# The last token tile's output product in two column halves, with its gate's products four places earlier in the order list

## Chip, cores and metric

One core of one Trainium2 chip runs the whole program. The metric is the device time of one execution in microseconds. Before the change three runs gave 260.70, 261.08 and 261.57 us, so the median is 261.08 us. One further execution was taken with the hardware profiler, and every instruction time below is from that one.

## What is computed

The inputs are `q`, `k`, `v`, `a_re`, `a_im` of shape (4, 8, 768, 48): batch, heads, sequence, head dimension. A complex gate `a`, capped at magnitude 0.999, drives a recurrence whose read-out `y` is `x` for a feed-forward part with a gated residual:

```python
S_re, S_im = (new_re + kv, new_im)                 # for each time step t
y[:, :, t] = np.einsum('bhd,bhde->bhe', q[:, :, t], S_re)
...
g, val = x @ w_gate, x @ w_val                     # x: 3072 tokens x 384
ffn_out = gelu(g) * val @ w_out                    # 384 -> 1536 -> 384
res_gate = 1.0 / (1.0 + np.exp(-(x @ w_res)))
return (x + res_gate * ffn_out).astype(np.float32)
```

The output is 3072 x 384 in float32.

## The kernel before

**Tiling.** The sequence is cut into chunks of 128 steps. One pair (batch, chunk) is a tile of 128 tokens, 24 in all. Tiles are worked on in 14 units, mostly two tiles at a time; the last two units hold one tile each: unit 12 is batch 2, chunk 5, and unit 13 is batch 3, chunk 5. `prepare` makes the decayed features of a unit, `attend` makes `x`, and `forward` makes the output. The loops over units call these three in turn, but that isn't the order in which instructions stand.

**The order.** Each call of `add` (L138) records a step: its engine, its kind, a function that issues its instructions, and the values that it reads and writes. Steps are numbered as they are recorded. `ORDER` (L41 to L105) is a list of these numbers, written out by hand, and `Plan.run` (L159) issues the steps in just that order. Each engine has its own queue, so a step's place matters against the other steps of its engine. `PLACE` (L30) maps some step numbers to an engine other than the one the code gives as a default. `Plan.run` also picks buffers: eight PSUM banks (`pb`) and three output tiles (`ot`) go round. For the kinds in `PORT` (L26), `otx` among them, it adds a wait that keeps such steps of DVE and of POOL one after the other. Waits between the engines are put in by the framework, from which tiles an instruction reads and writes.

**The end of `forward`** (L563 to L627), for one tile of 128 tokens:

- six rounds of gate and value products (L592, PE), GELU (L597, ACT) and gating (L598, DVE) give `h2`, 1536 x 128 in bf16;
- step kind `res`, three products with `wr` into a bank of its own (L607, PE), and `tanh` into `sg` (L609, ACT);
- step kind `out`, three steps of four products each (L618, PE), which add up in one bank of 128 x 384 float32. `lo` is 0, 4 and 8, and the third step closes the sum;
- step kind `ot`, the gate product `(sg + 1) * out` (L622, DVE). The factor one half of the sigmoid has been put into the gating of `h2`;
- step kind `otx`, the sum with `x` (L625, on POOL unless `PLACE` says DVE);
- step kind `store`, one DMA of 192 KB from SP's queue (L627).

The tile that finishes last is that of unit 12. `PLACE` puts its `otx` (step 1376) on DVE. The end of `ORDER` reads, with unit 13's steps (1378 and up) among unit 12's:

```
... 1445, 1368, 1443, 1369, 1372, 1446, 1373, 1447, 1370, 1448, 1374, 1371, 1449, 1375, 1376, 1377
```

Here 1372, 1373 and 1374 are the three `out` steps of unit 12, 1370 is its `res`, 1371 its `tanh`, 1375 its `ot`, 1376 its `otx` and 1377 its `store`. 1445 and 1446 are `out` steps of unit 13, 1447 is its `ot`, 1448 its `otx` and 1449 its `store`. On PE the last 23 products are therefore: unit 12 `lo` 0 and unit 13 `lo` 4 and 8 with unit 12 `lo` 4 (16 products in all), `res` of unit 12 (3), and unit 12 `lo` 8 (4).

After the last step the program closes: SP waits for every DMA semaphore and every engine's semaphore in turn, and then the engines meet at a barrier (all at the launching line, L665).

Of the kernel before, what the change touches and what calls it, by code (L numbers as in the profile page):

```python
# [15 lines left out]
OP = mybir.AluOpType  # L16
# [11 lines left out]


PLACE = {  # L30
    33: "DVE", 50: "DVE", 64: "ACT", 105: "DVE", 114: "DVE", 116: "POOL", 121: "DVE", 131: "DVE", 134: "ACT", 190: "DVE",
    191: "DVE", 213: "DVE", 221: "ACT", 223: "DVE", 225: "ACT", 230: "ACT", 245: "DVE", 305: "DVE", 306: "DVE", 323: "POOL",
    330: "DVE", 340: "DVE", 342: "ACT", 353: "DVE", 435: "ACT", 438: "ACT", 456: "DVE", 460: "DVE", 469: "DVE", 539: "DVE",
    551: "ACT", 554: "POOL", 555: "POOL", 562: "DVE", 570: "ACT", 572: "DVE", 576: "DVE", 599: "DVE", 654: "DVE", 667: "ACT",
    671: "POOL", 678: "DVE", 688: "DVE", 690: "ACT", 692: "DVE", 695: "ACT", 771: "DVE", 783: "ACT", 787: "POOL", 804: "DVE",
    806: "ACT", 811: "ACT", 817: "DVE", 831: "DVE", 872: "DVE", 899: "DVE", 902: "POOL", 903: "POOL", 943: "DVE", 1014: "POOL",
    1015: "POOL", 1022: "DVE", 1033: "ACT", 1041: "DVE", 1088: "DVE", 1124: "POOL", 1125: "POOL", 1143: "ACT", 1204: "DVE",
    1298: "DVE", 1314: "DVE", 1324: "ACT", 1325: "POOL", 1376: "DVE", 1386: "DVE", 1396: "ACT", 1397: "POOL", 1401: "DVE",
    1448: "DVE",
}  # L40
ORDER = [  # L41
# [63 lines left out]
]  # L105


# [19 lines left out]
class Plan:  # L127
# [10 lines left out]
    def add(self, eng, kind, fn, reads=(), writes=(), size=1, act=None):  # L138
        deps = set()
        for v in reads:  # L140
            deps.update(v.writers)
        for v in writes:
            deps.update(v.writers)
            deps.update(v.readers)
        stores = [v.store for v in list(reads) + list(writes) if v.store is not None]
        stores = sorted(set(stores), key=stores.index)
        t = Step(eng, kind, fn, deps, stores, size, act)
        t.index = len(self.steps)
        for v in writes:
            v.writers, v.readers = [t], []  # L150
        for v in reads:
            if t not in v.writers:
                v.readers.append(t)
        for x in stores:
            x.users.append(t)
        self.steps.append(t)
        return t
# [30 lines left out]
def kernel(  # L188
# [13 lines left out]
    nc = tc.nc  # L202
# [3 lines left out]
    DM = H * D  # L206
    FF = moe_w_gate.shape[1]
    KF = DM // 128
    NF = FF // 128
# [6 lines left out]
    NU = len(units)  # L216
    where = {bc: (p, i) for p, u in enumerate(units) for i, bc in enumerate(u)}
    size = [len(u) for u in units]

    ctx.enter_context(tc.manual_schedule())  # L220
    cst = ctx.enter_context(tc.tile_pool(name="cst", bufs=1))
# [26 lines left out]
    wo = cst.tile([128, NF, DM], BF, name="wo")  # L248
# [76 lines left out]
    on = {"DVE": nc.vector, "POOL": nc.gpsimd, "ACT": nc.scalar}  # L325
    add = plan.add

    def place(default):

        return PLACE.get(len(plan.steps), default)  # L330
# [6 lines left out]
    W = {}  # L337
# [226 lines left out]
    def forward(p):  # L564
        s, n = st[p], size[p]
        s["xT"], s["h2"] = Buf("xT"), Buf("h2")
        xT = [s["xT"].part() for _ in range(n)]
        for i in range(n):
            if p >= PE_X:
                add("SP", "dX", lambda i=i: nc.sync.dma_start(  # L570
                    out=s["xT"].tile[:, :, i, :], in_=s["x"].tile[:, i].rearrange("p h d -> p (h d)"), transpose=True), [s["xi"][i]], [xT[i]])
# [3 lines left out]
            def f(i=i, xp=xp):  # L575
                xp.make([128, KF, 128], BF)
                for k_ in range(KF):
                    nc.tensor.transpose(out=xp.tile[:, k_, :],
                                        in_=s["x"].tile[:, i].rearrange("p h d -> p (h d)")[:, k_ * 128:(k_ + 1) * 128], identity=ident)
# [3 lines left out]
        h2 = []  # L583
        for m in range(NF // 2):
            gp, vp, hh = Bank(), Bank(), s["h2"].part()
            h2.append(hh)
            for name, w_, o_ in (("wg", wg, gp), ("wv", wv, vp)):
# [11 lines left out]
                out=hv(), in0=hv(), scalar=0.5, in1=vp.tile, op0=OP.mult, op1=OP.mult), [vp], [hh], n)  # L599
        sg = [Buf("sg") for _ in range(n)]  # L600
# [9 lines left out]
                [rp], [sg[i]], 1, "G")  # L610
        for i, (b, c) in enumerate(units[p]):
            op_, ot = Bank(), Buf("ot")
            for lo in range(0, NF, 4):
                def f(i=i, lo=lo, op_=op_):
                    if lo == 0:
                        op_.make([128, DM])
                    for k_ in range(lo, lo + 4):
                        nc.tensor.matmul(out=op_.tile, lhsT=s["h2"].tile[:, k_, i * 128:(i + 1) * 128], rhs=wo[:, k_, :],  # L618
                                         start=(k_ == 0), stop=(k_ == NF - 1))
                add("PE", "out", f, [h2[lo // 2], h2[lo // 2 + 1], W["wo", lo]], [op_])  # L620
            ti = b * NC + c
            add("DVE", "ot", lambda i=i, op_=op_, ot=ot: nc.vector.scalar_tensor_tensor(  # L622
                out=ot.tile, in0=sg[i].tile, scalar=1.0, in1=op_.tile, op0=OP.add, op1=OP.mult), [sg[i], op_], [ot])
            e8 = place("POOL")
            add(e8, "otx", lambda i=i, ot=ot, e8=e8: on[e8].tensor_tensor(  # L625
                out=ot.tile, in0=ot.tile, in1=s["x"].tile[:, i].rearrange("p h d -> p (h d)"), op=OP.add), [s["xi"][i]], [ot])
            add("SP", "store", lambda ot=ot, ti=ti: nc.sync.dma_start(out=out[ti * 128:(ti + 1) * 128, :], in_=ot.tile), [ot], [])  # L627

    weights()
    for p in range(NU):  # L630
# [39 lines left out]
```

## Time and profile before

| what | value |
|---|---|
| median of three runs | 261.08 us (260.70 to 261.57) |
| the profiled execution | 261.98 us |
| its span, first to last instruction | 260.2 us |
| granted TensorE clock, mean | 0.974 |
| busy share PE, DVE, ACT, POOL | 85%, 87%, 81%, 35% |
| chain that ended last, by engine | PE 60%, DVE 19%, DMA 7%, SP's queue 5% |
| L618, `out` products 128x384, 288 of them | 55.5 us |
| L622, `ot` 128x384 on DVE, 24 of them | 13.1 us, 547 ns each |
| L625, `otx` 128x384 on POOL, 18 of them | 16.9 us, 941 ns each |
| L625, `otx` 128x384 on DVE, 6 of them | 556 ns each |
| stores on SP's queue, 24 of 192 KB | 2.5 us to landing (median) |

The profile follows one execution. PE, DVE, ACT and POOL are the compute engines, PEld is PE's weight load, SP issues DMAs, and a `q` behind an engine's name means its sequencer, which waits and issues. The chain of waits is followed back from the last instruction to whatever released each step. The timeline lists instructions with start and duration in microseconds.

### The profile page before, as it was taken

What the parts mean: (1) busy time and instruction counts of PE and PEld (TensorE: products, weight loads), DVE (VectorE), ACT (ScalarE), POOL (GpSimd) and SP (SyncE); (2) the same over time, 40 slices, a digit from 0 to 9 for tenths busy, and PEclk for the clock granted to TensorE, in tenths of its full rate; (3) what the DMA queues carried; (4) which work ended last, traced back from release to release, by engine and by line L of the source; (5) the groups of instructions that cost most, each with busy time, mean ns of one, the idle gap of its engine ahead of it and who ended that gap; (6) DMA issues with size and microseconds to landing.
All of it is one profiled execution on the core that took longest, in us unless ns stands there. A gap on an engine that the chain in (4) does not pass through costs nothing.

```text
span 260.2 us, 6343 instructions
## 1 busy us (share of the span) xinstructions
PE 222.3 (85%) x2415; PEld 174.7 (67%) x2415; DVE 225.7 (87%) x401; ACT 211.3 (81%) x354; POOL 90.4 (35%) x116
## 2 busy tenths in 40 slices
PE   0233842877999999999999999999999999999993
PEld 0011532757878877887887778768778778877881
DVE  2789999997999999999999999999999976573463
ACT  4899999998999999999999999797999932532330
POOL 1022266594611662486626177006020230101100
PEclk9999975799999999999999999999999999999999
DMA  8999999999999998999986779779789539201311
GB/s 140 188 186 186 188 185 167 205 181 217 152 183 185 164 199 161 192 178 183 214 147 121 153 155 168 181 145 232 131 134 222 97 88 170 75 3 35 113 40 60
DMA packets 162174, 39.83 MB, mean 153 GB/s; under 512 B 155616, under 2 KB 162144, under 8 KB 162144
## 3 DMA queue, kind: packets, MB, share of 16 engines
q1 hardware_dynamic: 157696, 35.53, 78.1%
q0 software_dynamic: 4448, 3.90, 9.7%
q8 instruction: 19, 0.31, 0.6%
q14 instruction: 11, 0.09, 0.1%
HBM read 31.26 MB, written 4.72 MB: 138 GB/s over the span
## 4 chain that ended last, share of the span: by engine, by line
PE 60%; DVE 19%; DMA 7%; SPq 5%; issue 4%; POOL 1%; ACT 0%; DVEq 0%; POOLq 0%; ACTq 0%
PE pb L592 30%; PE pb L618 16%; SPq L374 5%; PE pb L607 3%; PE pb L360 3%; PE pb L522 3%; DMA t<-fr 2%; PE pb L492 2%; DVE h L598 2%; DMA k<-in_k_dram 2%; DMA ai<-in_a_im_dram 2%; DVE fQ L475 2%; DVE Qe L470 2%; DVE ll L408 1%; DMA vf<-in_v_dram 1%
## 5 line engine op out<-in xcount | busy, mean ns | idle before, releaser
L597 ACT ACTIVATE h<-pb 128x512 bf16<-128x512 f32 (+1 forms) x84 | 41.1, 550 | 23.5 <-PE pb L592 23.1
L592 PE MATMUL pb<-xT,wg 128*128 128x256 bf16 (+1 forms) x504 | 56.0, 257 | 1.2 <-DVE U L552 0.9
L592 PE MATMUL pb<-xT,wv 128*128 128x256 bf16 (+1 forms) x504 | 57.0, 257 | 0.0
L618 PE MATMUL pb<-wo,h 128*128 128x384 bf16 x288 | 55.5, 326 | 0.0
L598 DVE SCALAR_TENSOR_TENSOR h<-h,pb 128x512 bf16<-128x512 bf16 (+1 forms) x84 | 48.0, 601 | 7.3 <-ACT h L597 4.6
L592 PEld LDWEIGHTS <-wg 128*128 128x128 bf16 x504 | 43.1, 98 | 8.1 <-issue 1.6
L592 PEld LDWEIGHTS <-wv 128*128 128x128 bf16 x504 | 42.2, 98 | 6.1
L639 ACT ACT_TABLE_LOAD x34 | 43.6, 1283 | 1.3 <-PEq L654 0.7
L525 DVE TENSOR_TENSOR am<-pb,mask 128x512 bf16<-128x512 f32 x48 | 31.6, 680 | 4.5 <-PE pb L522 4.3
L618 PEld LDWEIGHTS <-h 128*128 128x128 bf16 x288 | 26.0, 97 | 13.8 <-issue 0.3
L625 POOL TENSOR_TENSOR ot<-ot,x 128x384 f32<-128x384 f32 x18 | 16.9, 941 | 46.1 <-issue 19.9
L444 POOL TENSOR_TENSOR tl<-t,th 128x768 fp32r<-128x768 f32 (+1 forms) x9 | 13.2, 1479 | 22.7 <-DVE Gb L554 14.3
L522 PE MATMUL pb<-QT,KT 96*128 96x128 bf16 x192 | 16.7, 219 | 2.7 <-DVE KT L335 2.4
L622 DVE SCALAR_TENSOR_TENSOR ot<-sg,pb 128x384 f32<-128x384 f32 x24 | 13.1, 547 | 6.3 <-PE pb L618 6.2
L360 PE MATMUL pb<-lh,ut_hf 128*128 128x384 f16 x24 | 8.6, 360 | 11.1 <-DVE lh L406 11.1
L398 POOL TENSOR_TENSOR t<-t,ai 128x768 f32<-128x768 f32 (+1 forms) x9 | 14.7, 1637 | 8.8 <-DMA ai<-in_a_im_dram 3.5
L522 PEld LDWEIGHTS <-KT 96*128 96x128 bf16 x192 | 12.7, 97 | 6.5 <-DVE KT L335 2.9
L492 PE MATMUL pb<-ident,fK 128*128 128x128 bf16 x112 | 10.7, 252 | 6.8 <-DVE fK L475 6.0
L609 ACT ACTIVATE sg<-pb 128x384 f32<-128x384 f32 x24 | 11.9, 499 | 5.2 <-PE pb L607 3.2
L607 PE MATMUL pb<-wr,xT 128*128 128x384 bf16 x72 | 15.6, 326 | 0.3 <-DVE am L525 0.2
L334 ACT CAST x<-pb 128x384 bf16<-128x384 f32 x19 | 9.2, 482 | 6.4 <-PE pb L536 6.1
L360 PE MATMUL pb<-th,ut_hf 128*128 128x384 f16 x24 | 8.6, 359 | 6.4 <-DVE th L335 6.0
(89 smaller groups left out, 467.3 us busy)
## 6 DMA issues: line engine op xcount, KB each, us to landing
ar<-in_a_re_dram SPq DMA_DIRECT2D x24, 192.0 KB, 4.6
ai<-in_a_im_dram SPq DMA_DIRECT2D x24, 192.0 KB, 4.7
q<-in_q_dram SPq DMA_DIRECT2D x24, 192.0 KB, 4.6
k<-in_k_dram SPq DMA_DIRECT2D x24, 192.0 KB, 4.1
vf<-in_v_dram SPq DMA_DIRECT2D x24, 192.0 KB, 4.0
out_dram<-ot SPq DMA_DIRECT2D x24, 192.0 KB, 2.5
wg<-in_moe_w_gate_dram POOLq DMA_DIRECT2D x6, 192.0 KB, 7.1
wv<-in_moe_w_val_dram POOLq DMA_DIRECT2D x6, 192.0 KB, 6.2
```

Of the source, the lines that this page charges most:

```text
L360: nc.tensor.matmul(out=bank.tile, lhsT=ones, rhs=x[:, i * DM:(i + 1) * DM], start=(j == 0), stop=(j == 1))
L398: add(e1, "tai", lambda: on[e1].tensor_tensor(out=F("t"), in0=F("t"), in1=flat(T("ai"), n), op=OP.mult), [s["ai"]], [s["t"]], n)
L492: nc.tensor.transpose(out=tp.tile[:, h, :], in_=s[g].tile[:, i * H + h], identity=ident)
L522: nc.tensor.matmul(out=ap.tile[:, h, :], lhsT=kT.tile[0:DD, u * H // 2 + h, :], rhs=qT.tile[0:DD, u * H // 2 + h, :], start=True, stop=True)
L525: add("DVE", "am", lambda u=u, am=am, ap=ap: nc.vector.tensor_tensor(out=am.tile[:, u * H // 2:(u + 1) * H // 2, :], in0=ap.tile, in1=mask ...
L592: nc.tensor.matmul(out=o_.tile[:, u, :], lhsT=w_[:, k_, (2 * m + u) * 128:(2 * m + u + 1) * 128], rhs=s["xT"].tile[:, k_, 0:n].rearrange(" ...
L597: add("ACT", "gelu", lambda gp=gp, hv=hv: nc.scalar.activation(out=hv(), in_=gp.tile, func=AF.Gelu), [gp], [hh], n, "G")
L598: add("DVE", "h", lambda vp=vp, hv=hv: nc.vector.scalar_tensor_tensor(out=hv(), in0=hv(), scalar=0.5, in1=vp.tile, op0=OP.mult, op1=OP.mul ...
L607: nc.tensor.matmul(out=rp.tile, lhsT=s["xT"].tile[:, k_, i, :], rhs=wr[:, k_, :], start=(k_ == 0), stop=(k_ == KF - 1))
L618: nc.tensor.matmul(out=op_.tile, lhsT=s["h2"].tile[:, k_, i * 128:(i + 1) * 128], rhs=wo[:, k_, :], start=(k_ == 0), stop=(k_ == NF - 1))
L625: add(e8, "otx", lambda i=i, ot=ot, e8=e8: on[e8].tensor_tensor(out=ot.tile, in0=ot.tile, in1=s["x"].tile[:, i].rearrange("p h d -> p (h d ...
L639: plan.run(ORDER, lambda table: nc.scalar.preload_act_table_set(ACT_SETS[table]), after)
```

## The change

Only the tile of unit 12 (`TAIL = 12`) is treated differently. Its third `out` step becomes two steps of kind `outh`, each of four products over 192 of the 384 columns, into the two halves of the same bank. Then come two `ot` steps of 192 columns on DVE, two sums with `x` of a new kind `oth`, of 192 columns, the first on POOL and the second on DVE, and two stores of 128 x 192. `oth` isn't in `PORT`. Since unit 12 records four steps more, every later number in `ORDER` and `PLACE` goes up by four; the entry that put unit 12's `otx` on DVE is gone, and the new steps take the defaults. Beyond the numbering, the tail of `ORDER` changes: `res` and `tanh` of unit 12 (1370, 1371) now stand ahead of its second `out` step.

```diff
-    1437, 1357, 1442, 1365, 1366, 1445, 1368, 1443, 1369, 1372, 1446, 1373, 1447, 1370, 1448, 1374, 1371, 1449, 1375, 1376,
-    1377,
+    1441, 1357, 1446, 1365, 1366, 1449, 1368, 1447, 1369, 1372, 1450, 1370, 1371, 1373, 1451, 1452, 1374, 1375, 1453, 1376,
+    1377, 1378, 1379, 1380, 1381,
...
+            cols = [slice(0, DM)] if p != TAIL else [slice(0, DM // 2), slice(DM // 2, DM)]
+            acc, res = [op_], [ot]
             for lo in range(0, NF, 4):
...
+                if lo == NF - 4 and len(cols) > 1:
+                    acc, res = [Val(op_.store) for _ in cols], [Val(ot.store) for _ in cols]
+                    for x in acc:
+                        x.writers = list(op_.writers)
+                for x, sl in zip(acc, cols if len(acc) > 1 else [slice(0, DM)]):
+                    def f(i=i, lo=lo, op_=op_, sl=sl):
...
+                            nc.tensor.matmul(out=op_.tile[:, sl], lhsT=s["h2"].tile[:, k_, i * 128:(i + 1) * 128], rhs=wo[:, k_, sl],
+                                             start=(k_ == 0), stop=(k_ == NF - 1 and sl.stop == DM))
+                    add("PE", "out" if len(acc) == 1 else "outh", f, [h2[lo // 2], h2[lo // 2 + 1], W["wo", lo]], [x])
             ti = b * NC + c
...
+            for j, (x, y, sl) in enumerate(zip(acc, res, cols)):
+                add("DVE", "ot", lambda i=i, op_=op_, ot=ot, sl=sl: nc.vector.scalar_tensor_tensor(
+                    out=ot.tile[:, sl], in0=sg[i].tile[:, sl], scalar=1.0, in1=op_.tile[:, sl], op0=OP.add, op1=OP.mult), [sg[i], x], [y])
+            for j, (x, y, sl) in enumerate(zip(acc, res, cols)):
+                e8 = place("POOL" if j == 0 else "DVE")
+                add(e8, "otx" if len(cols) == 1 else "oth", lambda i=i, ot=ot, e8=e8, sl=sl: on[e8].tensor_tensor(
+                    out=ot.tile[:, sl], in0=ot.tile[:, sl], in1=s["x"].tile[:, i].rearrange("p h d -> p (h d)")[:, sl], op=OP.add), [s["xi"][i]], [y])
+            for j, (x, y, sl) in enumerate(zip(acc, res, cols)):
+                add("SP", "store", lambda ot=ot, ti=ti, sl=sl: nc.sync.dma_start(
+                    out=out[ti * 128:(ti + 1) * 128, sl], in_=ot.tile[:, sl]), [y], [])
```

In the new numbering 1374 and 1375 are the two `outh` steps, 1376 and 1377 the two gate products, 1378 (POOL) and 1379 (DVE) the two sums, 1380 and 1381 the two stores, and 1451, 1452 and 1453 are `ot`, `otx` and `store` of unit 13.

More of the change, by code (lines that the diff above doesn't have):

```diff
@@ L30 @@
 PLACE = {
[L31 to L39, printed above, removed]
+    33: "DVE", 50: "DVE", 64: "ACT", 105: "DVE", 114: "DVE", 116: "POOL", 121: "DVE", 131: "DVE", 134: "ACT", 190: "DVE", 191:
+    "DVE", 213: "DVE", 221: "ACT", 223: "DVE", 225: "ACT", 230: "ACT", 245: "DVE", 305: "DVE", 306: "DVE", 323: "POOL", 330:
+    "DVE", 340: "DVE", 342: "ACT", 353: "DVE", 435: "ACT", 438: "ACT", 456: "DVE", 460: "DVE", 469: "DVE", 539: "DVE", 551:
+    "ACT", 554: "POOL", 555: "POOL", 562: "DVE", 570: "ACT", 572: "DVE", 576: "DVE", 599: "DVE", 654: "DVE", 667: "ACT", 671:
+    "POOL", 678: "DVE", 688: "DVE", 690: "ACT", 692: "DVE", 695: "ACT", 771: "DVE", 783: "ACT", 787: "POOL", 804: "DVE", 806:
+    "ACT", 811: "ACT", 817: "DVE", 831: "DVE", 872: "DVE", 899: "DVE", 902: "POOL", 903: "POOL", 943: "DVE", 1014: "POOL", 1015:
+    "POOL", 1022: "DVE", 1033: "ACT", 1041: "DVE", 1088: "DVE", 1124: "POOL", 1125: "POOL", 1143: "ACT", 1204: "DVE", 1298:
+    "DVE", 1314: "DVE", 1324: "ACT", 1325: "POOL", 1390: "DVE", 1400: "ACT", 1401: "POOL", 1405: "DVE", 1452: "DVE",
 }
@@ L218 @@
     size = [len(u) for u in units]
+    TAIL = 12
     ctx.enter_context(tc.manual_schedule())
@@ L612, in forward @@
             op_, ot = Bank(), Buf("ot")
+            cols = [slice(0, DM)] if p != TAIL else [slice(0, DM // 2), slice(DM // 2, DM)]
+            acc, res = [op_], [ot]
             for lo in range(0, NF, 4):
[L614 to L619, printed above, removed]
@@ L620, in forward @@
-                add("PE", "out", f, [h2[lo // 2], h2[lo // 2 + 1], W["wo", lo]], [op_])
-            ti = b * NC + c
[L622 to L626, printed above, removed]
@@ L627, in forward @@
-            add("SP", "store", lambda ot=ot, ti=ti: nc.sync.dma_start(out=out[ti * 128:(ti + 1) * 128, :], in_=ot.tile), [ot], [])
+                if lo == NF - 4 and len(cols) > 1:
[4 more added lines that the diff above has]
+                    def f(i=i, lo=lo, op_=op_, sl=sl):
+                        if lo == 0:
+                            op_.make([128, DM])
+                        for k_ in range(lo, lo + 4):
+                            nc.tensor.matmul(out=op_.tile[:, sl], lhsT=s["h2"].tile[:, k_, i * 128:(i + 1) * 128], rhs=wo[:, k_, sl],
+                                             start=(k_ == 0), stop=(k_ == NF - 1 and sl.stop == DM))
+                    add("PE", "out" if len(acc) == 1 else "outh", f, [h2[lo // 2], h2[lo // 2 + 1], W["wo", lo]], [x])
```

46 rows, old and new, of the table ORDER are left out of this document.

## The prediction

> **What bounds the kernel now.** I read the chain of waits first, and of it only the end, since the change touches only the last tile.
>
> ```profile
> 253.88 0.81 PE pb L618 x5
> 254.69 0.49 PE pb L607 x3
> 255.18 0.66 PE pb L618 x4
> 255.84 0.04 DVEq L622
> 255.88 0.04 issue
> 255.93 0.56 DVE ot L622
> 256.49 0.02 issue
> 256.51 0.56 DVE ot L625
> ```
>
> PE runs without a gap to 255.84 us; then come the gate product, the sum with x and a store, one behind the other. What follows is in the timeline (first line: SP's queue), in the DMA view of 257.0 to 259.6 us (40 slices of 0.065 us), and in the closing waits of SP, line L665, asked for 257.2 to 258.2 and for 258.5 to 259.2 us:
>
> ```profile
> 257.10 0.33 SPq L627 DMA_DIRECT2D out_dram<-ot  x1
> ```
>
> ```profile
> DMA  0000000000000048999999520000000000000000
> out_dram<-ot SPq DMA_DIRECT2D x1, 192.0 KB, 1.9
> ```
>
> ```profile
> L665 SPq EVENT_SEMAPHORE  x9: 17/28/28, 257.5 to 258.0; - x9
> ```
>
> ```profile
> L665 SPq EVENT_SEMAPHORE  x1: 28/28/28, 259.0 to 259.0; - x1
> ```
>
> The store is issued at 257.10, its packets move from 257.91 to about 258.5 (0.6 us), it has landed 1.9 us after the issue, at 259.0, and the span ends 1.2 us later, at 260.2. Nine closing waits are through long before the landing, and a single one is left when it comes. So from PE's end there are 4.36 us of tail: 0.09 to the gate product, 1.14 to the sum's end, 0.03 to the store, 1.9 to the landing, 1.2 of closing. Only these can change.
>
> **Part 1, PE.** `res` and `lo` 4 swap places: three and four products of 0.163 us each (0.49/3, 0.66/4). Their sum stays. Neither waits: the last gating of h2 ends at 252.97 in the timeline, before either. The sixteen products ahead and unit 13's `ot`, `otx` and store keep their places. The tanh (0.49 us, from 255.22 to 255.71 before) ends about 0.65 us sooner, but it wasn't last: the gate product waited for PE to 255.84. If that cover went, nothing is lost, as the tanh only gets earlier. Gain 0. Four products of 384 columns become eight of 192. Products of 128 columns, each with its own weight load, stand in the chain at 6.70 us for 120, 0.056 each; at 384 it is 0.163. 192 lies on that line at 0.083, so eight take 0.66: cost +0.01 at most. Below nothing is excluded, the columns being the same.
>
> **Part 2, when the gate product can start.** The gain would be that the first half starts after four of the eight products, 0.33 us before PE's end. The built program speaks against it: of the two DVE gate products, the first waits for PE, ACT and a DMA, the second names no wait at all. The second needs the second half's products, so the first's wait already covers these. Both start after all eight. Gain 0.
>
> **Part 3, DVE.** One gate product of 0.553 and one sum of 0.557 become two of 192 columns and one of 192. The group rows have L598 (the same operation) at 410 ns for 256 columns and 678 for 512, 1.05 ns a column; so 192 takes 0.553 - 192 x 1.05 ns = 0.35 us, the sum 0.36. Independent DVE instructions of L598 follow each other closer than their duration (eight of 0.41 in 2.74 us, 0.34 apart, so 0.07 overlaps). First product 255.94 to 256.29, second 256.22 to 256.57, and its sum 256.59 to 256.95 if nothing stops it. That is 0.12 us earlier than before (257.07).
>
> **Part 4, POOL.** The first half's sum goes to an engine whose 128x384 sum has a median of 912 ns, and whose 128x768 subtraction (L444) takes 1641; 1.9 ns a column, so 192 takes 0.912 - 0.365 = 0.55 us (ends: 0.46, half of 912, and 0.91). From the end of a gate product on DVE to POOL's start the timeline has 0.12 (223.25 to 223.37), 0.13 (243.21 to 243.34) and 0.23 (238.59 to 238.82). With 0.13: start 256.42, end 256.97. SP follows a POOL end by 0.03 (239.73 to 239.76). So the first half store is issued at 257.00, only 0.10 before the whole one was.
>
> **Part 5, the second store behind the first on SP.** The added wait is the first store's for POOL, and the second store is queued behind it. Two stores that were both ready, one right behind the other:
>
> ```profile
> 245.94 0.33 SPq L627 DMA_DIRECT2D out_dram<-ot  x1
> ```
>
> ```profile
> 246.36 0.38 SPq L627 DMA_DIRECT2D out_dram<-ot  x1
> ```
>
> They are 0.42 apart, and the issue cost is the same for half a tile as far as the rows go (0.33 for 128 rows of 1536 bytes; 0.37 at the least for loads with 1024 rows of 192 bytes). So the second store is issued at 257.42, 0.32 later than before. DVE's half, ready at 256.95, waits 0.47 there. Of the 1.9 us to landing 0.6 are packets. Half the bytes take 0.3 at the same rate; the loads' packets of 192 bytes take 20.6 ns each by queue q1's share (78.1% of 16 engines over 260.2 us, 157,696 packets), those of 1536 bytes 0.6 x 16/128 = 75 ns, so 768 bytes lie near 44 ns or 0.35 us for 128 packets on 16 engines. Landing after 1.9 - 0.6 + 0.35 = 1.65 (ends 1.6 and 1.9): at 259.07, against 259.0. Net **+0.07** (ends -0.1 and +0.45).
>
> **Part 6, the closing waits.** The DMA semaphores of SP's queue are eight, taken in turn. The last store of before has number 7, and the closing waits go from 0 to 7, so only its own was left at the landing. The change adds one DMA: the last store now has number 0 (its row in the built program waits for DMAHW0, where the half before it waits for DMAHW7). Numbers 1 to 7 are then waited for after it has landed. The nine closing waits quoted run from 257.5 to 258.0, by their starts 0.06 apart. Seven more behind the landing cost 7 x 0.06 = **+0.42** (ends: 0, should they be taken faster when all are met; 0.45).
>
> **Sum.** 0.01 + 0.07 + 0.42 = +0.50 us. The profiled execution took 261.98, its span 260.2 and 1.78 around it, which nothing here touches: 262.48. It is 0.90 above the median of the runs shown, 261.08; the tail doesn't hang on that, so on the median's scale I forecast **261.6**. The bounds of the terms give -0.1 to +0.9.
>
> **A rule that speaks against the change.** While POOL's sum ran from 243.34, a gate product ran on DVE from 243.37:
>
> ```profile
> 243.34 0.91 POOL L625 TENSOR_TENSOR ot<-ot,x 128x384 f32<-128x384 f32 x1 [3.62 <-issue]
> 243.37 0.55 DVE L622 SCALAR_TENSOR_TENSOR ot<-sg,pb 128x384 f32<-128x384 f32 x1 [0.15 <-PE pb L618]
> ```
>
> Both took what they take alone. But there DVE read one operand from PSUM. DVE's second sum reads both from SBUF, and no row shows that beside a POOL sum, since `PORT` keeps those apart and `oth` isn't in it. The Trainium skill, page "SBUF — State Buffer", section "Who interferes with whom", says that a VectorE instruction with two SBUF inputs contends with a GpSimd instruction that reads SBUF, and that the second to start is blocked until the first is through. The pair quoted agrees with its other half, that one SBUF input doesn't contend. By that rule, if POOL is first (256.42 against 256.59), DVE's sum runs from 256.97 to 257.33, still ahead of the second store's turn at 257.42: the sum stays.
>
> **Rivals.**
> 1. *DVE takes the operands first* (slower): if POOL starts later than 256.59, 0.30 and not 0.13 after the first product (the longest gap seen is 0.23), and the two then exclude each other, POOL's sum starts at 256.97 and ends at 257.52, the stores go at 257.55 and 257.97, the landing is at 259.62, the closing 0.42 later: +1.05 us, **262.1**. Against it: the gap must be longer than any row's. Chance 0.13. The rule of the Trainium skill's page "SBUF — State Buffer" would give just this.
> 2. *The closing waits cost nothing*, or the second store lands a little sooner: +0.1 us, **261.2**. For it: the waits' spacing was seen while nothing waited behind them. Chance 0.20.
> 3. *The first half does start early*, though the built waits say otherwise: first product at 255.61, POOL's sum 256.09 to 256.64, stores at 256.67 and 257.09, landing 258.74, closing 0.42 later: +0.16, **261.2**. Not faster even so. Chance 0.05.
> 4. *The halves gain*: a POOL sum of 0.46, a store that lands in 1.6, closing for nothing: -0.1, and with a lucky draw of runs faster by more. Chance 0.04.
>
> The forecast has the rest, 0.58.
>
> **Chances and range.** Runs of this kernel differ by 0.87 us, and about 0.3% (0.78 us) is what a measurement can tell from no change. The forecast's +0.5, with 0.35 for its terms and for a median of few runs, passes +0.78 in a fifth of its cases (0.12); rival 1 does in nearly all (0.12); the others hardly (0.02). Slower 0.26, faster 0.03, within 0.3% 0.71. The range takes in rivals 2 and 3 below and rival 1 above: 260.9 to 262.3.
>
> **What would show it.** In the profile after: the two gate products start 0.28 apart behind PE's end (Part 2; 0.3 before it, and rival 3 holds). The first sum on POOL takes 0.55 and its store goes near 257.0 if the rest of the span is unmoved (Part 4). The two stores are 0.42 apart, and PE's end to the last landing is 3.23 us against 3.16 (Part 5). After the last landing seven or eight closing waits of L665 instead of one, and 1.6 us to the end of the span instead of 1.2 (Part 6). PE's end to the end of the span is 4.9 us against 4.36. It is wrong if POOL starts after DVE's sum, if half a store lands as late as a whole one, or if the span before 253 us moves, which nothing in the change asks for: no other instruction changes its place.

## The result, and the profile after

The changed kernel takes 261.79 us (median of nine runs, 261.58 to 262.29) against 260.72 us for the kernel before (nine runs, 260.33 to 261.57): a ratio of 1.0041, 95% interval 1.0029 to 1.0054, or 1.07 us slower. The forecast was 0.5 us slower, with 1.05 us as a rival by another mechanism.

The two profiled spans, 260.2 and 260.3 us, must not be compared as they stand. The profiled execution of before took 261.98 us, 1.26 above the median of its kernel, and PE's last product ended there at 255.84 us, after the change at 254.87. What the change touches lies behind that point, so I compare the **tail**, from PE's end to the end of the span: 4.37 us before, 5.45 after, a difference of 1.08 that agrees with the 1.07 of the timed runs.

The end of the chain of waits, after (start, duration, what):

```profile
253.07 0.49 PE pb L607 x3
253.55 1.32 PE pb L625 x12
254.88 0.04 DVEq L630
254.91 0.04 issue
254.96 0.63 DVE ot L630 x2
255.59 0.02 issue
255.61 0.55 DVE ot L634
```

All twelve last products run in one piece (four of 384 columns and eight of 192), `res` (L607) ahead of them, and the two gate products start 0.09 us behind PE's end and follow each other. The timeline has the two sums and the two stores:

```profile
255.39 0.55 POOL L634 TENSOR_TENSOR ot<-ot,x 128x192 f32<-128x192 f32 x1 [12.11 <-DVE ot L630]
255.61 0.55 DVE L634 TENSOR_TENSOR ot<-ot,x 128x192 f32<-128x192 f32 x1
255.97 0.33 SPq L637 DMA_DIRECT2D out_dram<-ot  x1
256.39 0.38 SPq L637 DMA_DIRECT2D out_dram<-ot  x1
```

The DMA view of 255.9 to 258.5 us shows the packets of the two stores one behind the other, and their landing time:

```profile
DMA  0000000000000059997202899841000000000000
out_dram<-ot SPq DMA_DIRECT2D x2, 96.0 KB, 1.7
```

So the last landing is at 256.39 + 1.7 = 258.09. Then come the closing waits of SP (line L676 now, asked for 257.5 to 258.67 us):

```profile
L676 SPq EVENT_SEMAPHORE  x8: 28/28/28, 258.1 to 258.5; - x8
L676 SPq DRAIN  x2: 7/10/13, 258.6 to 258.7; - x2
```

Eight waits instead of one stand behind the landing, and SP is through at 258.66. In the kernel before, SP was through at 259.11 and the barrier began at once, at 259.14. Here it begins at 259.26, 0.60 us after SP, and the reason is a row of the launching line that the prediction leaves out, POOL's closing drain. First POOL's drain and its steps at the barriers after the change, then the same before it:

```profile
L676 POOLq DRAIN  x1: 3857/3857/3857, 255.4 to 255.4; - x1
L676 POOLq EVENT_SEMAPHORE  x4: 17/17/17, 259.3 to 260.2; - x4
```

```profile
L665 POOLq DRAIN  x1: 4212/4212/4212, 243.3 to 243.3; - x1
L665 POOLq EVENT_SEMAPHORE  x4: 17/17/17, 259.1 to 260.1; - x4
```

The drain's record begins just before POOL's last sum starts (255.36 against 255.39) and goes on well past that sum's end. After the change the last sum ends at 255.94 and the drain at 255.355 + 3.857 = 259.21, which is 3.27 us later. Before, the last sum ended at 244.26 and the drain at 247.53, also 3.27 later, hidden under more than eleven microseconds of other engines' work. DVE's closing drain shows nothing of the kind: before the change it ended at 257.12, 0.05 us after DVE's last sum. The change brings the end of POOL's last instruction from 14.7 us to 2.15 us ahead of the last landing, and the barrier waits for the drain.

### The profile page after: what moved, and what is told of

Its sections match the earlier page's. It is cut to its first block, busy times and chain, and to the rows that moved or that the text cites. A ratio compares the mean times of both kernels' runs of the same rounds, so it can differ in the third digit from the quotient of the medians.

```text
span 260.3 us, 6356 instructions
## 1 busy us (share of the span) xinstructions
PE 222.1 (85%) x2419; PEld 175.0 (67%) x2419; DVE 225.3 (87%) x402; ACT 211.4 (81%) x354; POOL 90.8 (35%) x117
## 4 chain that ended last, share of the span: by engine, by line
PE 68%; DVE 15%; DMA 6%; SPq 5%; issue 3%; POOL 1%; DVEq 0%; POOLq 0%
PE pb L592 34%; PE pb L625 17%; SPq L374 5%; PE pb L607 4%; PE pb L360 3%; PE pb L522 3%; DMA t<-fr 2%; DMA k<-in_k_dram 2%; PE pb L492 2%; DMA ai<-in_a_im_dram 2%; DVE h L598 2%; DVE Qe L470 1%; DVE fQ L475 1%; PE pb L536 1%; PE pb L534 1%
## 5 line engine op out<-in xcount | busy, mean ns | idle before, releaser
L625 PE MATMUL pb<-wo,h 128*128 128x384 bf16 (+1 forms) x292 | 55.5, 324 | 0.0
L634 POOL TENSOR_TENSOR ot<-ot,x 128x384 f32<-128x384 f32 (+1 forms) x19 | 17.4, 917 | 57.9 <-DVE ot L630 29.0
L630 DVE SCALAR_TENSOR_TENSOR ot<-sg,pb 128x384 f32<-128x384 f32 (+1 forms) x25 | 13.1, 529 | 6.0 <-PE pb L625 6.0
L398 POOL TENSOR_TENSOR t<-t,ai 128x768 f32<-128x768 f32 (+1 forms) x9 | 14.7, 1635 | 8.8 <-DMA ai<-in_a_im_dram 3.6
L607 PE MATMUL pb<-wr,xT 128*128 128x384 bf16 x72 | 15.6, 326 | 0.3 <-DVE am L525 0.2
```

The source lines that it names most:

```text
L398: add(e1, "tai", lambda: on[e1].tensor_tensor(out=F("t"), in0=F("t"), in1=flat(T("ai"), n), op=OP.mult), [s["ai"]], [s["t"]], n)
L607: nc.tensor.matmul(out=rp.tile, lhsT=s["xT"].tile[:, k_, i, :], rhs=wr[:, k_, :], start=(k_ == 0), stop=(k_ == KF - 1))
L625: nc.tensor.matmul(out=op_.tile[:, sl], lhsT=s["h2"].tile[:, k_, i * 128:(i + 1) * 128], rhs=wo[:, k_, sl], start=(k_ == 0), stop=(k_ == N ...
L634: add(e8, "otx" if len(cols) == 1 else "oth", lambda i=i, ot=ot, e8=e8, sl=sl: on[e8].tensor_tensor(out=ot.tile[:, sl], in0=ot.tile[:, sl] ...
```

## The experiments

Tail is taken from each run's one profile; the ratio is to the kernel before on the same chip, with its 95% interval.

| run | tail, us | ratio |
|---|---|---|
| kernel before | 4.37 | |
| changed kernel | 5.45 | 1.0041 (1.0029 to 1.0054) |
| e1 both sums on DVE | 4.75 | 1.0025 (1.0015 to 1.0036) |
| e2 undivided sum on POOL | 6.01 | 1.0066 (1.0050 to 1.0082) |
| e3 one early store split | 4.90 | 1.0032 (1.0020 to 1.0043) |
| e4 tiny late POOL copy, new tile | 5.99 | 0.9994 (0.9980 to 1.0009) |
| e5 the same copy, no new tile | 6.00 | 1.0052 (1.0033 to 1.0071) |
| e6 tiles 32 bytes higher | 4.33 | 0.9929 (0.9911 to 0.9948) |
| e7 order alone | 4.36 | 1.0014 (0.9998 to 1.0031) |
| e8 two banks, one store | 4.02 | 0.9988 (0.9978 to 0.9999) |
| e9 halves on DVE, one store | 4.34 | 0.9985 (0.9966 to 1.0004) |
| e10 eight early stores split | 4.48 | 1.0036 (1.0011 to 1.0060) |
| e11 tiles 64 bytes higher | 4.31 | 1.0005 (0.9987 to 1.0023) |
| e12 two banks and 32 bytes | 4.02 | 0.9909 (0.9886 to 0.9933) |

**e1: the changed kernel with no late POOL sum.** `PLACE` gets `1378: "DVE"`.

> The changed kernel with the first half's sum on DVE instead of POOL; everything else of the change stays. Theory A (POOL's closing drain): POOL's drain ends 3.3 us after POOL's last instruction and holds the barrier in the changed kernel; with no late POOL instruction it ends long before, and what is left is SP's path: the second store is issued 1.46 us after PE's end, has landed 1.70 later, and seven closing waits behind it cost 0.43. So 0.45 us above the kernel before (0.3 to 0.6), 0.6 below the changed kernel. Rival B (the sums and stores are what costs, POOL and DVE taking operands from each other): DVE's sum loses its 0.19 us of contention, but the second store's turn on SP is later than that anyway, so it stays about 1.05 us above the kernel before.

Tail 4.75, 0.70 less than with POOL's half, and 0.25% over the kernel before. POOL's drain began at 242.2 in this run and lasted 4211 ns, long over when SP came through. SP's path is as I had priced it: eight closing waits behind the landing are still there (257.9 to 258.3), and the tail is 0.38 above that of the kernel before. The time is 0.62 us above it by the medians (interval 0.39 to 0.94), a little over the 0.3 to 0.6 expected; what it has beyond the tail, if anything, wasn't traced. Theory A holds; B, which wanted 1.05, falls.

**e2: the kernel before with its last sum on POOL.** The entry `1376: "DVE"` is taken out of `PLACE`.

> The kernel before with one thing changed: the last tile's sum with x, undivided, on POOL instead of DVE. Theory A: POOL's sum ends about 1.69 us after PE's end, its drain 3.3 us later, at 4.99, where the barrier was met at 3.30 after PE's end before: 1.7 us slower than before (1.5 to 1.9). Rival B: only the sum and the store are later, 1.72 us after PE's end instead of 1.26: 0.46 slower.

1.72 us slower by the medians (262.33 against 260.61), tail 1.64 longer, where the later store alone would be 0.46. The view of L665 has POOL's drain reach from 255.37 to 259.59, 3.27 behind the sum's end, while SP is through at 258.36:

```profile
L665 POOLq DRAIN  x1: 4219/4219/4219, 255.4 to 255.4; - x1
```

**e3: only the semaphore of the last store.**

```diff
-            add("SP", "store", lambda ot=ot, ti=ti: nc.sync.dma_start(out=out[ti * 128:(ti + 1) * 128, :], in_=ot.tile), [ot], [])
+            def put(ot=ot, ti=ti, parts=(2 if p == 3 and i == 0 else 1)):
+                w = DM // parts
+                for j in range(parts):
+                    nc.sync.dma_start(out=out[ti * 128:(ti + 1) * 128, j * w:(j + 1) * w], in_=ot.tile[:, j * w:(j + 1) * w])
+            add("SP", "store", put, [ot], [])
```

> The kernel before with one early store (the first tile of unit 3, over 150 us ahead of the end) issued as two halves of the columns, so that the last store has DMA semaphore 0 instead of 7. Nothing at the end of the program is touched. Theory (closing waits in a fixed order): seven more waits are left when the last store lands, 0.06 us each: 0.43 us slower than before (0.3 to 0.5). Rival: waits that are already met cost nothing, or one more DMA costs nothing: no change, within 0.1 us.

The closing waits stand behind the landing as foreseen, from SP's view of L669:

```profile
L669 SPq EVENT_SEMAPHORE  x8: 28/28/28, 258.2 to 258.6; - x8
```

The time is 0.61 us higher by the medians, and the interval (0.52 to 1.12 us) lies above the 0.43 expected. The tail is 0.53 longer, of which 0.41 is SP's coming through later and 0.1 lies in POOL's clearing between the barriers. So the waits are real. Whether some tenths more lie ahead of the tail is not shown: the interval begins where the tail's 0.53 is.

**e4: a tiny POOL copy at the end.** `nc.gpsimd.tensor_copy(out=late, in_=last[0].tile[:, 0:1])` behind the last sum, from the last output tile into a new 128x1 tile `late`.

> The kernel before with one instruction more: POOL copies one column (128x1) of the last output tile into a tile that nothing reads, after the last sum on DVE. No result and no store waits for it. Theory A (the drain runs from POOL's last instruction, whatever its size): the copy ends about 1.5 us after PE's end, the drain 3.3 us later at 4.8, where the barrier was met at 3.30 before: 1.5 us slower (1.3 to 1.7). If the drain is longer for larger instructions, less, down to 0.2. Rival B (the drain isn't on the path): no change.

This looked like a failure of theory A: no change in the time. But the tail had grown by 1.62 us, as the theory says, while PE's end came at 252.70, 2 to 3 us earlier than in any kernel so far. Instructions and waits ahead of the tail were the same. What differed was that the new tile moved the tiles allocated after it, all the working tiles, by 32 bytes. (Such places are worked out here from the tiles' sizes, which the framework rounds up to 32 bytes; the traces carry no addresses.) So the run had two effects, and the next two take them apart.

**e5: the same copy into a column that exists.** `late` becomes `zero`, whose last reader is long done.

> The tiny late POOL copy once more, but into a column that was there already, so that every tile keeps its place in SBUF; it is one instruction more than the kernel before and nothing else. In the run with a new tile the traced tail behind PE's end was 1.6 us longer, as theory A says, while the time was unchanged, because PE's end came earlier. If that came from the new tile (all later tiles moved by 32 bytes), this run shows theory A's price alone: 1.6 us slower than before (1.4 to 1.8). If a late POOL instruction is free, no change.

0.52% slower, 1.36 us (0.86 to 1.85), tail 1.63 longer. The drain behind a 0.19 us copy ends as late after it as the drain behind a sum of 128x384: it begins at 256.13, the copy ends at 256.34, and the drain at 256.13 + 3.48 = 259.62, 3.27 behind the copy.

```profile
L669 POOLq DRAIN  x1: 3482/3482/3482, 256.1 to 256.1; - x1
```

**e6: the tiles 32 bytes higher, nothing else.**

```diff
+    late = cst.tile([128, 1], FP, name="late")
```

Nothing reads or writes this tile.

> The kernel before with one unused 128x1 tile in the constants' pool: the instructions and waits of every engine are the same, only the tiles that are allocated after it lie 32 bytes higher. If the places of the tiles matter, 1.7 us faster than before (1.3 to 2.1) with the tail of 4.37 us unchanged. Rival: places don't matter, and the earlier end of PE was of another cause: no change.

1.83 us faster (0.71%) with the same instructions and waits. The DMA view shows what else differs, first before, then this run, queue q1 (packets, MB, share of 16 engines) and a load:

```profile
q1 hardware_dynamic: 157696, 35.53, 78.1%
...
ai<-in_a_im_dram SPq DMA_DIRECT2D x24, 192.0 KB, 4.7
```

```profile
q1 hardware_dynamic: 157696, 35.53, 67.8%
...
ai<-in_a_im_dram SPq DMA_DIRECT2D x24, 192.0 KB, 3.9
```

The same packets and bytes take 14% less of the DMA engines' time (78.1% of 260.2 us against 67.8% of 257.5). That the faster transfers are what shortens the program is argued, not shown; no wait was followed from them to PE's end. e4, which has the same tile and the late copy besides, is 1.7 us slower than this run by the ratios, and its tail is 1.66 longer: theory A's price once more. None of this is part of the change, which adds no tile.

**e7: the order alone.** Only the tail of `ORDER` is changed (`res` two places earlier, its `tanh` four), nothing is divided.

> The kernel before with the changed order of the last steps alone (the gate's products and tanh ahead of the second product step), nothing divided. All theories: no change within 0.1 us; tail behind PE's end 4.37 us. If the order cost something of its own, slower.

Tail 4.36; the time's interval reaches from -0.02% to +0.31%. The tail shows that the moved products cost nothing there; the time alone leaves it unclear. e9 below has the same order and is not slower than the kernel before.

**e8: the halves really early.** Each half gets a bank of its own (all three product steps divided), both sums are on DVE, and one store takes the whole tile.

> The last tile in two halves, each in a bank of its own so that the first gate product waits only for the first half's products; both sums on DVE, one whole store. By the accounts of theory A and of the closing waits nothing late is left on POOL and the last store keeps semaphore 7: the first gate product starts 0.24 us before PE's end, the store is issued 0.98 us after it instead of 1.26, tail 4.1 instead of 4.37: 0.2 us faster than before (0 to 0.4). Rival (dividing costs in itself): slower, as the changed kernel is.

```profile
253.22 1.00 PE pb L623 x12
254.23 0.03 DVEq L632
254.26 0.04 issue
254.31 0.63 DVE ot L632 x2
254.94 0.27 DVE ot L636
```

The twelve products of 192 columns in the chain end at 254.22 and the first gate product starts at 254.31. The other half's last four products, 0.08 us each, come behind those twelve and end at 254.55, so the gate product starts 0.24 us before PE's end, as expected. The store goes 0.95 us behind PE's end (1.26 before), tail 4.02, time 0.12% less (0.01 to 0.22%).

**e9: divided work, undivided store.** As the changed kernel with both sums on DVE, but one DMA for both halves.

> The changed kernel with both sums on DVE and the two halves stored by one DMA: products, gate products and sums stay divided. If the closing waits and POOL's drain are all that the change costs, nothing is left of it: the store is issued 1.27 us after PE's end against 1.26, keeps semaphore 7, tail 4.4 us: no change against the kernel before (within 0.2), 0.45 below the run with both sums on DVE and two stores. Rival (dividing the products or the DVE work costs): 0.3 us or more slower than before.

Tail 4.34, no difference in time. Both gate products start behind PE's end again. Dividing costs nothing and gains nothing here; what e1 has above this run is the second store with its closing waits.

**e10: eight early splits.** The condition of e3 becomes `3 <= p <= 6`.

> The kernel before with eight early stores (units 3 to 6) issued as two halves each, eight DMAs more, so that the last store has semaphore 7 again. By the theory of the closing waits this costs nothing at the end, tail 4.37 us, where one split cost 0.5 to 0.6: no change (within 0.3, if eight more issues on SP are hidden). Rival (each DMA more costs by itself): slower than with one split.

One closing wait is left behind the landing again, and SP is through 3.27 us after PE's end, as before. But the time is 0.36% up, so my expectation of no change fails: the eight extra DMAs cost about 0.9 us (0.3 to 1.6). The tail is only 0.11 longer, so by subtraction most of it lies ahead of PE's end; where, wasn't traced. That is also why e3's price can't be read from its time alone.

**e11: the tiles 64 bytes higher.** As e6, with a tile of 128x16.

> The kernel before with an unused tile of 64 instead of 4 bytes in the constants' pool, so that the later tiles lie 64 bytes higher, where the 32 bytes gave 1.8 us. If what counts is that load targets start at a multiple of 64 bytes (they are 32 past one in the kernel before, and again here), no change, and the loads land in 4.6 us as before. Rival (any other place, or more distance): as fast as with 32 bytes.

No change, the loads of `a` and `q` land in 4.6 us as before. With 32 bytes more the load targets start at a multiple of 64 bytes, with 64 more they are 32 past one, as in the kernel before. Both runs agree with that reading, but all working tiles moved, not the load targets alone: in e6 the transposes into `xT` also went from 3.8 to 2.9 us. Other distances weren't tried.

**e12: both gains.** e8 with the unused tile of e6.

> The two-bank version with one store and the unused 4-byte tile as well. If the two gains are independent they add: 1.8 and 0.3, so 2.1 us faster than before (1.6 to 2.6), with a tail of 4.05 us.

258.85 us against 261.10, ratio 0.9909 (0.9886 to 0.9933): faster than both kernels, tail 4.02 as in e8. That is 2.25 us by the medians (interval 1.75 to 2.98) against the expected 2.1: within the noise the gains add.

## Why the prediction was right and where it failed

The time lay in the range and on the forecast side, but the rise was about twice the forecast, and the likeliest class, within 0.3%, was not what came: 0.41%. Luck had a part in it. The bounds of the terms ended at +0.9 us, and the range reached further only for the sake of rival 1, which did not happen. And 261.6 came as near to 261.79 as it did because the kernel before has a median of 260.72 us over nine runs, not the 261.08 of the three shown. Point by point:

- **Parts 1 and 2** held. PE runs through, the products of 192 columns are 0.083 us apart, and both gate products start behind the last product of the second half. With a bank for each half (e8) the first starts 0.24 us before PE's end; in e9, with one bank and the same division of the last products and of DVE's work, it starts 0.09 us behind it. So one bank for both halves was what held it.
- **Part 3, DVE**: 0.35 us a gate product as worked out. The second sum took 0.545 us beside POOL's sum and 0.350 without it (e1), so it ended 1.28 us behind PE's end instead of 1.11. As foreseen, this hid under the first store's turn on SP. It is the pair of operands of the rule I weighed. The Trainium skill, "SBUF — State Buffer", section "Who interferes with whom", has the second of such a pair blocked until the first is through. An estimate by that rule starts the sum at POOL's end (255.94) and ends it at 256.29. The trace agrees in part: the sum ended at 256.15, so it was held up, but, as far as POOL's recorded end goes, by less than the whole of POOL's time.
- **Part 4, POOL**: 0.547 us, forecast 0.55; it started 0.08 us after the first gate product, forecast 0.13, and the first store went 1.10 us behind PE's end, forecast 1.16.
- **Part 5**: stores 0.42 apart, landing 3.22 us behind PE's end, forecast 3.23. Two small errors cancel there: the second store went 0.06 earlier than forecast and took 1.70 to land instead of 1.65.
- **Part 6**: the seven waits cost 0.42 us on SP, as forecast, though not in the time of this kernel.
- **The sum failed by a missing term.** I let the closing begin when SP is through and took the 1.2 us after the landing as fixed. For SP alone the sum was right: SP is through 3.79 us behind PE's end against 3.27 before, +0.52 where +0.50 was forecast. But the barrier waits for every engine, and POOL, whose drain had been over at 247.53, now drains until 259.21, 0.55 us after SP. 0.52 and 0.55 make the 1.07, and the drain alone sets where it ends. The row that shows such a drain was in the profile of before, 4212 ns from 243.3 on; the prediction reads only SP's rows of that line.
- **Which of the two prices counts**: they lie side by side, so the later one decides. In the changed kernel the closing waits are hidden behind POOL's drain, and undoing them alone would gain nothing as long as the sum is on POOL. That follows from the two ends, 258.66 and 259.21; it wasn't run by itself, but e2 and e5, which have one closing wait behind the landing and a late POOL instruction, also end by POOL's drain.
- **Rivals**: the first gave nearly the measured time by a mechanism that did not happen (POOL started 0.22 us ahead of DVE's sum, not behind it). A right number would have hidden a wrong cause. The second, third and fourth did not come.
- **Signs of being wrong**: the landing is 2.23 us ahead of the end of the span, not 1.6, for the most part by the missing term. Another named sign appeared too: the span ahead of 253 us moved, and PE's end came 0.97 us earlier. e5, which is the kernel before but for one copy at the end, has PE's end at 254.85 as well, so I take this for the variation between executions and not for an effect of the change.

Left open: what an early split store costs ahead of the tail (e3, e10), how the place of a transfer's target slows its packets, and why POOL's drain takes 3.27 us.

## What to carry to other kernels

When an instruction is moved onto an engine that had been finished for long, look up in the profile how long that engine's closing drain takes after its last instruction, and add it to the time at which the instruction will end. In this kernel, dividing the last tile pays only if the halves may start apart (a PSUM bank for each) and if what is added at the end, another DMA and its turn in the closing waits, isn't longer than what is saved. Compare tails from a common point in two profiles, and keep an eye on the tiles' places: a new tile that nothing uses moved this kernel by more than the change did.

## What the hardware showed that I had not expected

- POOL's closing drain ends 3.27 to 3.28 us after its last instruction in every one of the fourteen profiles, whether that is a sum of 128x384 (e2), of 128x192 (the changed kernel) or a copy of 128x1 (e5).
- With the working tiles moved by 32 bytes, by their sizes to a multiple of 64 (e6), the 192 KB loads of `a` and `q`, in rows of 192 bytes, land in 3.9 us instead of 4.6 to 4.7, those of `k` and `v` in 3.9 and 3.8 instead of 4.1 and 4.0, and queue q1's share falls from 78.1% to 67.8%; with 64 bytes (e11) they land as before.
- A DVE sum with both operands in SBUF took 0.545 us beside a POOL sum instead of the 0.350 of e1, a delay of 0.2 us, shorter than the 0.33 us for which POOL's sum was still recorded as running when it started.
